# A fused window attention and two-layer network: the order of the first token tile's attention, its value products and its bank order

## The chip, the core and the metric

The kernel runs on one core of one Trainium2 chip. The core has five engines that each work through a queue of their own in order: TensorE (PE, matrix products; PEld in the profile is its weight load), VectorE (DVE), ScalarE (ACT), GpSimd (POOL) and SyncE (SP). They meet through semaphores. Data lies in SBUF, 128 partitions wide; products are written to PSUM, which the kernel uses as eight banks of 128 x 512 float32. DMA transfers are issued from POOL and SP (one from ACT at the very end). The metric is device time in microseconds (us) for one launch.

## The reference

Batch 8, 8 heads, 576 positions, 64 numbers a head. Each query sees the 64 keys up to and including its own position. The attention's output, 4608 rows of 512, goes through a layer of 2048 columns, `h * cos(h)`, and a layer back to 512.

```python
def _attn_ref(q, k, v):
    scores = scale * np.matmul(q, k.transpose(0, 1, 3, 2))
    rel = pos[:, None] - pos[None, :]
    mask = (rel >= 0) & (rel < 64)
    scores = np.where(mask, scores, -1000000000.0)
    ...
    return np.matmul(attn, v).astype(np.float32)

def _moe_ref(x, w_in, w_out):
    h = x @ w_in
    g = h * np.cos(h)
    return (g @ w_out).astype(np.float32)
```

## The kernel before

**Tiling.** The 4608 rows are cut into nine token tiles of 512 rows (`mt`). A tile's input `xT` (512 numbers deep, 512 rows wide, turned) comes from the attention as four slices, one for each pair of heads (`p` = 0 to 3). The first layer makes 16 column blocks (`ff`) of 128, each from four products of 128 x 128 by 128 x 512, one for each pair (`first`, line 351). ACT takes the cosine as a sine with an offset (line 519), DVE multiplies it with `h` (line 522), and the second layer sums 16 products for each 128 rows (line 534).

**Attention.** Queries come in blocks of 64 (`j` = 0 to 8). A block `j` needs the keys of blocks `j - 1` and `j`, so a unit is one pair and one block with 128 keys. The first token tile is batch 0, blocks 0 to 7. Its 32 units are handled in eight groups of four: group `p.g` is pair `p`, blocks `4g` to `4g + 3`. The steps of a group have letters, and so do the steps of a pair:

- `tq.p`, `tk.p`: 18 turns on PE each (line 186) of a pair's queries or keys into a PSUM tile of tag `t` (three buffers). `pq.p`, `pk.p`: its copy to SBUF on DVE (`d`) or ACT (`a`), lines 193 to 199.
- `s.p.g`: one product that lays the mask into a bank (line 238) and eight scores (line 244). `m`: the maximum, negated, on DVE (line 273). `e`: four exponentials with their sums on ACT, read from the score bank itself (line 288). `i`: the reciprocal on DVE (line 295). `n`: the multiply into weights `w` on POOL (`p`) or DVE (`d`), line 302.
- `w.p.g`: four turns of the weights on PE into a `t` tile (line 311); `c.p.g`: its copy to SBUF (`wT`).
- `v.p`: 16 products of weights and values (line 330) into a `t` tile; `x.p`: its copy into `xT`.
- `z.half`: the spread of the values. They are loaded in chunks of 128 rows into the even ones of eight slots. A block with odd `j` finds its two key blocks in one slot, `j - 1`. A block with even `j` needs the upper half of one chunk and the lower half of the next; for it the odd slots are filled by two copies, `z.1` (upper halves, POOL) and `z.0` (lower halves, DVE).
- `l`: the next of seven loads on POOL: three parts of `w_in`, `q` and `k` of batch 1, two halves of `w_out`.
- `h.p`: the share of pair `p` in the first three column blocks, `hx.f`: pairs 0 and 1 of column block `f`, `hl`: pairs 2 and 3 of the first five column blocks. `tb` loads the sine table on ACT.

**What sets the order.** The string `FIRST` (lines 41 to 48) is the order by hand of everything up to the first layer of tile 0; line 490 walks through it and issues each step to its engine's queue. Behind it come the loads of batch 0's last values and batch 1's values (lines 493 to 495). Then the loop over the tiles runs from line 497, and a plan with due times (`at`, `pump`) puts the attention of the next batches between the products. The turns of batch 1's `q` and `k` are due at 7 to 12.7 (lines 424 to 427), from the eighth column block of tile 0 on.

**Banks.** Five PSUM banks have names (O0, O1, X0, X1, S), three are the tag `t`. `S_FIRST` (line 101) names the banks of the scores in turn, and `H_FIRST` (line 96) those of the 16 column blocks of tile 0. A bank is used again only when the last reader of its contents is done. `skew(mt)` is the number of column blocks that are begun before all four pairs are there: five for tiles 0 and 1, three (`SKEW`) for the others.

Of the kernel before, what the change touches and what calls it, by code (L numbers as in the profile page):

```python
# [10 lines left out]
def _safe_warn(msg, *a, **kw):  # L11
# [14 lines left out]
GF = 4  # L26
# [25 lines left out]
def kernel(  # L52
# [43 lines left out]
    H_FIRST = ("O1", "X0", "X1", "S", "O0") * 3 + ("X0",)  # L96
# [208 lines left out]

    def g_trans(n):
# [27 lines left out]

    def put_x(mt, p, engine=None):
# [18 lines left out]
    def skew(mt):  # L354
        return 5 if mt < 2 else SKEW
# [118 lines left out]
    def load():  # L474
# [7 lines left out]
             "mk": put_masks, "ck": lambda: cast("k", "d"), "l": load, "tb": sine_table, "h": lambda p: skewed(0, p, next(turn_h)), "hl": lambda: last_pairs(0),  # L482
             "hx": lambda ff: [first(0, ff, ks, ks == 0, False) for ks in range(2)],
             "z": lambda half, engine=None: spread_v(0, half, engine),
# [3 lines left out]
             "c": lambda p, g, engine=None: g_put(2 * p + g, engine), "v": lambda p: values(0, p),  # L488
# [4 lines left out]
    load_v(0, 4)  # L493
    for c in range(5):
        load_v(1, c)
# [81 lines left out]
```

## Time and profile before

| | us |
|---|---|
| three runs | 305.22, 307.27, 306.64 |
| median | 306.64 |
| the profiled execution, its time | 306.41 |
| its span, first to last instruction | 304.4 |
| PE busy in the span | 288.7 (95%) |
| ACT busy | 235.7 (77%) |
| DVE busy | 220.4 (72%) |
| POOL busy | 171.1 (56%) |

The page divides the span into 40 slices of 7.6 us and gives each engine's busy tenths there. A row of the timeline has the start, the length, the engine, the line, the operation, what it writes and reads with shapes, and how many were merged; in brackets is the engine's idle time ahead of it and what ended that. A row of a group has the count, the time in all, the mean in ns, and the idle time ahead. A row of DMA issues has the queue, the count, the size and the median time to landing. By windows, the profile gives each engine's busy time in a stretch, with the granted clock of PE, from 0 to 1, near its end. The window 30 to 40 us has PE busy for 9.44 of 10 us, the windows of 50 us behind 50 us for 49.4 to 49.5.

### The profile page before, as it was taken

Reading aid. Unit: us, or ns where it says so; the run is one execution under the profiler, and the core shown is the slowest. Engines: PE = TensorE matmul, PEld = TensorE weight load, DVE = VectorE, ACT = ScalarE, POOL = GpSimd, SP = SyncE. Lnnn points to the kernel's source line nnn. Section 1 sums busy time; section 2 is a strip of 40 time slices with the busy share of each in tenths; the row PEclk is TensorE's granted clock in tenths of the full one; section 3 lists DMA queues with packets and bytes.
Section 4 is the critical chain, followed back from the end, with each engine's and each line's share of the span. In section 5 each row is a group of like instructions: output and inputs, shape, how many; then the busy total and the mean of one; then the engine's idle time right before and its main releaser. Section 6 shows DMA issues by size and latency. Waiting matters only on the chain.

```text
span 304.4 us, 7847 instructions
## 1 busy us (share of the span) xinstructions
PE 288.7 (95%) x2628; PEld 142.1 (47%) x2668; DVE 220.4 (72%) x834; ACT 235.7 (77%) x786; POOL 171.1 (56%) x198
## 2 busy tenths in 40 slices
PE   3769999999999999999999999999999999999996
PEld 3544444544454445444544444444444454454443
DVE  3896889588787878787877787778778877236701
ACT  5997799967997799779987998799869986106600
POOL 8996257977774976497659665967433630000000
PEclk9989999999999999999999999999999999999999
DMA  7999999699969999999999979999994441011012
GB/s 150 181 211 207 207 155 139 105 165 191 225 114 155 225 164 132 154 201 183 138 167 208 189 106 172 157 219 123 180 172 110 87 130 62 0 72 70 0 69 71
DMA packets 165577, 43.88 MB, mean 144 GB/s; under 512 B 154720, under 2 KB 160800, under 8 KB 165536
## 3 DMA queue, kind: packets, MB, share of 16 engines
q0 software_dynamic: 99344, 18.06, 75.1%
q1 hardware_dynamic: 66048, 25.11, 40.2%
q8 instruction: 21, 0.34, 0.5%
q14 instruction: 20, 0.16, 0.2%
q10 hardware_dynamic: 144, 0.20, 0.2%
HBM read 36.70 MB, written 9.44 MB: 152 GB/s over the span
## 4 chain that ended last, share of the span: by engine, by line
PE 88%; DVE 6%; issue 2%; ACT 2%; DMA 1%; POOL 0%; DVEq 0%; POOLq 0%
PE h_ps L351 41%; PE out_ps L534 36%; PE o_ps L330 3%; PE s_ps L261 3%; DVE negm L273 1%; PE out_ps L371 1%; DMA first_f<-in_q_dram 1%; DVE w L302 1%; PE tq_ps L186 1%; DVE s L277 1%; DVE v L109 1%; PE tk_ps L186 1%; PE tw_ps L311 1%; PE s_ps L244 1%; ACT e L288 1%
## 5 line engine op out<-in xcount | busy, mean ns | idle before, releaser
L351 PE MATMUL h_ps<-xT,w_in 128*128 128x512 bf16 x556 | 127.1, 381 | 2.2 <-DVE xT L109 0.6
L534 PE MATMUL out_ps<-w_out,gT 128*128 128x512 bf16 x543 | 123.0, 379 | 1.8 <-issue 1.1
L522 DVE TENSOR_TENSOR gT<-h_ps,sin 128x512 bf16<-128x512 f32 x144 | 95.4, 688 | 33.6 <-ACT sin L519 33.4
L519 ACT ACTIVATE sin<-h_ps 128x512 f32<-128x512 f32 x144 | 82.9, 599 | 34.1 <-PE h_ps L351 32.8
L288 ACT ACTIVATE e<-s,negm 128x128 f32<-128x128 f32 x256 | 98.6, 388 | 0.3 <-DVE negm L277 0.3
L302 POOL TENSOR_TENSOR w<-e,rden 128x512 bf16<-128x512 f32 (+1 forms) x76 | 74.5, 993 | 31.5 <-DVE rden L295 29.1
L351 PEld LDWEIGHTS <-w_in 128*128 128x128 bf16 x576 | 56.0, 98 | 67.1 <-issue 2.7
L534 PEld LDWEIGHTS <-gT 128*128 128x128 bf16 x560 | 53.2, 98 | 62.4 <-issue 0.2
L277 DVE CUSTOM_DVE_ANT_0 s<-s_ps,mask 128x128 f32<-128x128 f32 x256 | 58.0, 284 | 0.1
L288 ACT ACTIVATION_READ_ACCUMULATOR e<-s,negm 128x1 f32 x256 | 48.1, 188 | 0.0
L149 POOL DMA_DIRECT2D rows<-in_q_dram x30 | 25.4, 867 | 25.9 <-DMA T<-rows 16.6
L162 POOL DMA_DIRECT2D v<-in_v_dram x35 | 29.8, 879 | 10.5 <-DMA rows<-in_k_dram 7.3
L109 ACT COPY out_sb<-out_ps 128x512 f32<-128x512 f32 (+1 forms) x18 | 10.1, 563 | 24.2 <-PE out_ps L534 18.7
L295 DVE RECIPROCAL rden<-den 128x4 f32<-128x4 f32 (+1 forms) x80 | 13.8, 172 | 19.2 <-ACT e L288 18.6
L149 POOL DMA_DIRECT2D rows<-in_k_dram x30 | 25.5, 897 | 2.2 <-DMA T<-rows 2.2
L109 DVE CAST xT<-o_ps 128x512 bf16<-128x512 f32 x27 | 17.6, 679 | 6.5 <-PE o_ps L330 6.3
L277 DVE DVE_READ_ACCUMULATOR2_ANT negm<- 128x1 f32 x256 | 21.2, 83 | 0.0
L109 DVE COPY out_sb<-out_ps 128x512 f32<-128x512 f32 x18 | 12.4, 689 | 12.0 <-PE out_ps L534 12.0
L288 ACT ACTIVATE e<-s_ps,negm 128x128 f32<-128x128 f32 x32 | 11.5, 425 | 1.6 <-DVE negm L273 1.6
L261 PE MATMUL s_ps<-T 64*64 64x128 bf16 x512 | 12.1, 221 | 0.0
L261 PEld LDWEIGHTS <-T 64*64 64x64 bf16 x512 | 8.2, 106 | 8.3 <-DVE negm L277 4.4
L330 PEld LDWEIGHTS <-v 128*64 128x64 bf16 x504 | 9.5, 112 | 4.3 <-issue 2.1
(56 smaller groups left out, 146.2 us busy)
## 6 DMA issues: line engine op xcount, KB each, us to landing
out_dram<-out_sb SPq DMA_DIRECT2D x16, 512.0 KB, 6.1
v<-in_v_dram POOLq DMA_DIRECT2D x28, 128.0 KB, 8.3
rows<-in_q_dram POOLq DMA_DIRECT2D x24, 128.0 KB, 5.2
rows<-in_k_dram POOLq DMA_DIRECT2D x24, 128.0 KB, 7.8
w_out<-in_moe_w_out_dram POOLq DMA_DIRECT2D x2, 1024.0 KB, 16.7
w_in<-in_moe_w_in_dram POOLq DMA_DIRECT2D x2, 768.0 KB, 12.4
wT<-w SPq DMA_TRANSPOSE x66, 3.9
out_dram<-out_sb SPq DMA_DIRECT2D x3, 256.0 KB, 2.0
```

The lines of the kernel that those rows point to most:

```text
L109: {"a": nc.scalar.copy, "p": nc.gpsimd.tensor_copy}.get(engine, nc.vector.tensor_copy)(out, in_)
L149: nc.gpsimd.dma_start(out=rows(b)[lo:lo + n, slot * 512:slot * 512 + 512].rearrange("p (h d) -> p h d", h=H), in_={"q": q, "k": k}[name][b ...
L162: nc.gpsimd.dma_start(out=vt.rearrange("p (h d) -> p h d", h=H), in_=v[b, :, c * 128:c * 128 + n, :].rearrange("h p d -> p h d"))
L261: nc.tensor.matmul(out=s_ps[cross][to, u].rearrange("p (a t) -> p a t", a=2), lhsT=q_cols(b, p, j)[d], rhs=k_cols(b, p, j)[d], start=True, ...
L277: nc.vector.tensor_tensor_reduce(out=s[:, u], in0=s_ps[:, u], in1=mask[:, 2 - j % 2 if j else 0], scale=-scale if b else -1.0, scalar=BIG, ...
L288: nc.scalar.activation(e[:, u], s[:, u], AF.Exp, bias=negm[:, u:u + 1], scale=1.0 if n < n_first else -1.0, accum_out=den[:, u:u + 1])
L302: (nc.gpsimd if engine == "p" else nc.vector).tensor_tensor(out=w[:, 0:u], in0=e[:, 0:u], op=ALU.mult, in1=rden[:, 0:u].unsqueeze(2).to_br ...
L330: nc.tensor.matmul(out=o_ps[64 * h:64 * h + 64, 64 * i:64 * i + 64], lhsT=values_of(b)[:, max(j - 1, 0), 128 * p + 64 * h:128 * p + 64 * h ...
L351: nc.tensor.matmul(out=st["h", ff], lhsT=w_in_sb[:, ks, ff * 128:ff * 128 + 128], rhs=st["xT", mt][:, ks], start=start, stop=stop)
L519: nc.scalar.activation(sin, h_ps, AF.Sin, bias=math.pi / 2.0)
L522: nc.vector.tensor_tensor(out=gt[:, e], in0=h_ps, in1=sin, op=ALU.mult)
L534: nc.tensor.matmul(out=o_ps[e], lhsT=gT[ff // 2][:, ff % 2, ms * 128:ms * 128 + 128], rhs=w_out_sb[:, ff], start=ff == 0, stop=ff == n_ff - 1)
```

## The change

The order `FIRST` is written anew. What else changes belongs to steps in it:

- `warm.24` stands first: 24 products of the identity with itself (128 x 128 by 128 x 128) into bank X1, which nothing reads.
- Both scores, maxima and exponentials of pair 0 come ahead of pair 1's copies; before, `s.0.1 tq.1 tk.1 s.0.0` and `m.0.0` came later.
- `pk.3` and `c.1.0` go from ACT to DVE, `c.2.0` too; `n.1.0` from DVE to POOL; `x.0` from DVE to ACT. Of `n.3.1` DVE makes three units and POOL the fourth (`nh`).
- The loads `l` are issued at other places: one as before, two behind `n.0.1`, the last four behind `nh.3.1`.
- Values of pairs 0 and 1 don't use the odd slots: `va.p` makes the products of the odd blocks from one slot, as before, and those of the even blocks with the lower half; `vb.p` adds the even blocks' upper half from the chunk before. That is 24 products for a pair and not 16. They go to banks X0 and S and not to a `t` tile. The spread `z` covers pairs 2 and 3 alone, half the columns, and `spread_last` copies slot 7's upper half for pairs 0 and 1 behind the loads of `l`, for tile 1.
- `h` begins two column blocks and not three, `hx` one and not two, `hl` ends three and not five, and `H_FIRST` has another order for the first ten column blocks.
- `tb` moves from behind `w.3.1` to behind the last copy into `xT`.

```diff
 FIRST = (
-    "tq.0 mk ck tk.0 pq.0.d pk.0.a s.0.1 tq.1 tk.1 l s.0.0 m.0.1 pq.1.d tq.2 e.0.1 pk.1.d s.1.0 pq.2.a "
-    "tk.2 s.1.1 i.0.1 tq.3 l m.0.0 m.1.0 pk.2.d n.0.1.p s.2.0 l w.0.1 tk.3 s.2.1 e.0.0 l e.1.0 m.1.1 "
-    "l i.0.0 e.1.1 pq.3.d i.1.0 m.2.0 pk.3.a e.2.0 n.0.0.p n.1.0.d z.1.p w.0.0 i.1.1 m.2.1 e.2.1 "
-    "s.3.0 s.3.1 c.0.1.d n.1.1.p c.0.0.d w.1.0 m.3.0 i.2.0 z.0.d c.1.0.a n.2.0.p w.1.1 c.1.1.d v.0 "
-    "i.2.1 v.1 n.2.1.p m.3.1 e.3.0 e.3.1 l x.0.d w.2.0 i.3.0 x.1.d h.0 c.2.0.a n.3.0.p w.2.1 h.1 hx.3 "
-    "i.3.1 n.3.1.d w.3.0 c.2.1.a w.3.1 tb v.2 c.3.0.d x.2.a c.3.1.d v.3 l x.3.d hx.4 hl "
+    "warm.24 tq.0 mk ck tk.0 pq.0.d pk.0.a s.0.1 s.0.0 tq.1 tk.1 l m.0.1 e.0.1 m.0.0 e.0.0 pq.1.d tq.2 tk.2 pk.1.d "
+    "s.1.0 pq.2.a s.1.1 i.0.1 n.0.1.p l l m.1.0 e.1.0 tq.3 pk.2.d i.0.0 n.0.0.p s.2.0 w.0.1 m.1.1 e.1.1 tk.3 s.2.1 "
+    "pq.3.d i.1.0 n.1.0.p z.1 m.2.0 pk.3.d e.2.0 w.0.0 i.1.1 n.1.1.p m.2.1 e.2.1 "
+    "c.0.1.d s.3.0 s.3.1 z.0 i.2.0 n.2.0.p m.3.0 e.3.0 c.0.0.d w.1.0 va.0 i.2.1 n.2.1.p m.3.1 e.3.1 w.1.1 "
+    "c.1.0.d i.3.0 n.3.0.p c.1.1.d w.2.0 w.2.1 c.2.0.d va.1 vb.0 i.3.1 nh.3.1 l l l l x.0.a c.2.1.a w.3.0 "
+    "c.3.0.d w.3.1 c.3.1.d h.0 vb.1 x.1.d v.2 x.2.a v.3 h.1 hx.2 x.3.d tb hl "
 )
...
-    H_FIRST = ("O1", "X0", "X1", "S", "O0") * 3 + ("X0",)
+    H_FIRST = ("O1", "X0", "O0", "S", "X1") * 2 + ("O1", "X0", "X1", "S", "O0", "X0")
...
+    def spread_pairs(half):
+        vt = values_of(0)[:, :, d_model // 2:]
+        if half:
+            nc.gpsimd.tensor_copy(vt[64:128, 1:8:2], vt[64:128, 0:7:2])
+        else:
+            nc.vector.tensor_copy(vt[0:64, 1:7:2], vt[0:64, 2:8:2])
+
+    def spread_last():
+        vt = values_of(0)[:, :, 0:d_model // 2]
+        nc.gpsimd.tensor_copy(vt[64:128, 7], vt[64:128, 6])
...
+    def g_norm_halves(n):
...
+        for engine, lo, hi in ((nc.vector, 0, 3), (nc.gpsimd, 3, 4)):
+            engine.tensor_tensor(out=w[:, lo:hi], in0=e[:, lo:hi], op=ALU.mult,
+                                 in1=rden[:, lo:hi].unsqueeze(2).to_broadcast([128, hi - lo, 128]))
...
+    def warm(n):
+        to = bank("X1", "none_ps")
+        for _ in range(n):
+            nc.tensor.matmul(out=to[:, 0:128], lhsT=ident, rhs=ident, start=True, stop=True)
+
+    def values_first(p, part):
+        if part == "a":
+            st["o", 0, p] = bank(("X0", "S")[p], "o_ps")
+        lower, upper, both = slice(0, 64), slice(64, 128), slice(0, 128)
+        parts = {"a": [(lower, j, j) for j in range(0, TU, 2)] + [(both, j - 1, j) for j in range(1, TU, 2)],
+                 "b": [(upper, max(j - 2, 0), j) for j in range(0, TU, 2)]}[part]
...
     def skew(mt):
-        return 5 if mt < 2 else SKEW
+        return 5 if mt == 1 else SKEW
...
-        for ff in range(skew(mt) if mt else SKEW):
+        for ff in range(skew(mt) if mt else 2):
...
     load_v(0, 4)
+    spread_last()
     for c in range(5):
         load_v(1, c)
```

More of the change, by code (lines that the diff above doesn't have):

```diff
@@ L304, in g_norm @@
         st["w", n] = w
+    def g_norm_halves(n):
+        (e, _), rden = st.pop(("e", n)), st.pop(("r", n))
+        w = att.tile([128, GF, 128], BF16, tag="w", name="w", bufs=8)
+        for engine, lo, hi in ((nc.vector, 0, 3), (nc.gpsimd, 3, 4)):
+            engine.tensor_tensor(out=w[:, lo:hi], in0=e[:, lo:hi], op=ALU.mult,
+                                 in1=rden[:, lo:hi].unsqueeze(2).to_broadcast([128, hi - lo, 128]))
+        st["w", n] = w
     def g_trans(n):
@@ L332, in values @@
                                  rhs=wT[:, 64 * (h ^ cross):64 * (h ^ cross) + 64], start=True, stop=True, skip_group_check=True)
+    def warm(n):
[8 more added lines that the diff above has]
+                 "b": [(upper, max(j - 2, 0), j) for j in range(0, TU, 2)]}[part]
+        for i, (ks, slot, j) in enumerate(parts):
+            for h in range(2):
+                nc.tensor.matmul(out=st["o", 0, p][64 * h:64 * h + 64, 64 * j:64 * j + 64],
+                                 lhsT=values_of(0)[ks, slot, 128 * p + 64 * h:128 * p + 64 * h + 64],
+                                 rhs=st["wT", (0, p, j)][ks, 64 * h:64 * h + 64],
+                                 start=part == "a" and i == 0, stop=True, skip_group_check=True)
     def put_x(mt, p, engine=None):
@@ L487 @@
              "n": lambda p, g, engine: g_norm(2 * p + g, engine), "w": lambda p, g: g_trans(2 * p + g),
-             "c": lambda p, g, engine=None: g_put(2 * p + g, engine), "v": lambda p: values(0, p),
+             "c": lambda p, g, engine=None: g_put(2 * p + g, engine), "va": lambda p: values_first(p, "a"), "vb": lambda p: values_first(p, "b"), "v": lambda p: values(0, p),
+             "z": spread_pairs,
              "x": lambda p, engine=None: put_x(0, p, engine)}
```

4 lines of the change are left out of this document (2 added, 2 removed).

## The prediction

> **What bounds the kernel now.** I read the page first: its span, and TensorE and its clock in 40 slices.
>
> ```profile
> span 304.4 us, 7847 instructions
> PE   3769999999999999999999999999999999999996
> PEclk9989999999999999999999999999999999999999
> ```
>
> TensorE (PE) is full from the fifth slice on; only the first three, some 23 us, have holes, and the change edits little else. So I went to the chain of waits (start, length, what), for where the full stretch begins.
>
> ```profile
> 20.59 0.59 PE h_ps L351
> 24.64 0.61 PE o_ps L330 x24
> 25.74 0.59 PE h_ps L351 x2
> 26.36 4.69 PE h_ps L351 x21
> ```
>
> From 26.36 the first-layer products run back to back, 4.69 / 21 = 0.22 us apart. The first token tile needs 64 of them. Ten stand ahead of `hl` in the old order (3 in each `h`, 2 in each `hx`), so 54 are left at 26.36. The question is when the new order starts its dense run, and with how many left. Then I read the front in the timeline, engine by engine.
>
> ```profile
> 7.73 0.37 ACT L288 ACTIVATE e<-s_ps,negm 128x128 f32<-128x128 f32 x1 [1.45 <-DVE negm L273]
> 9.82 0.65 ACT L197 ACTIVATE T<-tq_ps 128x576 bf16<-128x576 bf16 x1 [0.58 <-PE tq_ps L186]
> 10.36 0.36 ACT L288 ACTIVATE e<-s_ps,negm 128x128 f32<-128x128 f32 x1
> 14.47 0.71 ACT L109 COPY T<-tk_ps 128x576 bf16<-128x576 bf16 x1
> 17.73 0.72 ACT L109 COPY wT<-tw_ps 128x512 bf16<-128x512 bf16 x1
> 21.42 0.59 ACT L109 COPY wT<-tw_ps 128x512 bf16<-128x512 bf16 x1
> 11.58 0.81 POOL L175 DMA_DIRECT2D w_in<-in_moe_w_in_dram  x1
> 12.38 0.75 POOL L142 DMA_DIRECT2D rows<-in_q_dram  x1
> 13.11 0.76 POOL L142 DMA_DIRECT2D rows<-in_k_dram  x1
> 13.87 1.07 POOL L302 TENSOR_TENSOR w<-e,rden 128x512 bf16<-128x512 f32 x1
> 15.00 2.25 POOL L109 COPY v<-v 64x2048 bf16<-64x2048 bf16 x1
> 21.46 1.06 POOL L302 TENSOR_TENSOR w<-e,rden 128x512 bf16<-128x512 f32 x1
> 13.96 1.53 DVE L302 TENSOR_TENSOR w<-e,rden 128x512 bf16<-128x512 f32 x1
> 21.79 1.29 DVE L302 TENSOR_TENSOR w<-e,rden 128x512 bf16<-128x512 f32 x1
> 25.62 0.69 DVE L109 CAST xT<-o_ps 128x512 bf16<-128x512 f32 x1 [0.41 <-PE o_ps L330]
> ```
>
> ScalarE (ACT) makes the exponentials of eight groups between 7.73 and 21.42. Twelve of them lie without a gap between 10.36 and 14.47, 0.343 apart, so 32 take 11.0. GpSimd (POOL) has its first weights done early but starts `n.0.0` only at 13.87, behind three transfers, and later carries the 2.25 us spread. From the last exponential (21.4) to the last `xT` cast's end (26.3) are 4.9 us. That tail and the two queues ahead of it are what the change rewrites.
>
> **ACT's queue.** Ahead of the last exponential the old order has 11.0 of exponentials, `pq.2` (0.65), `pk.3` (0.71), `c.1.0` (0.72) and a 0.58 wait. The change takes `pk.3` and `c.1.0` to VectorE (DVE) and puts `e.0.0` in the wait. Left are 11.0 + 0.65, so the last exponential ends at 7.73 + 11.65 = 19.4, if no maximum is late.
>
> **DVE's queue.** It takes those two, and `c.2.0`, and gives away `n.1.0`, a quarter of `n.3.1`, half of `z.0` and one cast of `xT`.
>
> ```profile
> L273 DVE TENSOR_REDUCE negm<-s_ps 128x4 f32<-128x512 f32 x8 | 5.4, 672 | 1.7 <-PE s_ps L244 1.7
> L199 DVE TENSOR_SCALAR T<-tq_ps 128x576 bf16<-128x576 bf16 x3 | 2.2, 743 | 0.3 <-PE tq_ps L186 0.3
> L109 DVE COPY wT<-tw_ps 128x512 bf16<-128x512 bf16 x5 | 1.9, 416 | 1.4 <-PE tw_ps L311 1.4
> L109 DVE COPY v<-v 64x1536 bf16<-64x1536 bf16 x1 | 1.5, 1482 | 0.0
> L295 DVE RECIPROCAL rden<-den 128x4 f32<-128x4 f32 x8 | 1.4, 170 | 0.6 <-ACT e L288 0.6
> ```
>
> From `m.0.1` (7.0; its result fed the exponential at 7.73) to `m.3.1` it now has eight maxima (5.4), five copies of turned rows (3.7), two of `wT` (0.8), half a spread (0.75) and six reciprocals (1.0): 11.7, so 18.7 at full lengths one behind the other. The exponentials of `3.1` could begin at 19.4 - 1.4 = 18.0. So the cover is thin: between nothing and 0.7 goes to ACT. I take the middle, 0.3, and the last exponential ends at 19.7.
>
> **POOL's queue.** Weights `0.1` can start at 9.8: their reciprocal stands behind two maxima and two copies, 7.0 + 2 x 0.67 + 2 x 0.74. Then come 1.05 of multiply and two transfers of 0.81, so 12.5. From there six multiplies at 1.06 and the half spread, 2.25 / 2 = 1.1, end at 20.0. So POOL, not ACT, releases the last group, 2.5 us before the old `n.3.0` ended (21.46 + 1.06). `n.3.1` follows: three quarters on DVE, one on POOL. In the old trace DVE's multiplies stretched to 1.53 and 1.29, and both ended 0.55 after POOL's own multiply did (15.49 against 14.94, 23.08 against 22.52). So DVE stood still until POOL was through and then needed 0.55. I price the split in series: 0.27 + 0.75 x 0.55 = 0.7, ending at 20.7; its ends are 0.41 (side by side) and 1.15 (three quarters of 1.53). The Trainium skill, "SBUF — State Buffer", section "SBUF: two separate sides", says that a DVE operation with two SBUF inputs and a GpSimd operation reading SBUF take a shared port pair as an exclusive lock. It speaks against this split: by it DVE alone would need 0.55 and the split at least as much, whereas a shared bandwidth would give 0.41.
>
> **The tail on PE.** After `w.3.1` PE runs, in its order: `h.0` (2 products), `vb.1` (8), `v.2`, `v.3` (16 each), `h.1`, `hx.2` (2 each), then `hl`.
>
> ```profile
> 21.83 0.63 PE L311 MATMUL tw_ps<-ident,w 128*128 128x128 bf16 x4
> 22.25 1.94 PE L351 MATMUL h_ps<-xT,w_in 128*128 128x512 bf16 x5
> 24.57 1.01 PE L330 MATMUL o_ps<-wT,v 128*64 128x64 bf16 x32
> 16.83:20.24 3.41, 1.68 (x42) 1.22 (x41) 3.41 (x7) 3.23 (x18) 3.33 (x4) 1.00 1.16 211
> 20.24:23.65 3.41, 2.84 (x10) 1.40 (x11) 2.43 (x5) 2.91 (x11) 3.39 (x5) 0.50 1.17 210
> ```
>
> The last two rows are windows (length, PE, PEld, DVE, ACT, POOL, granted clock, DMA share, GB/s). After the thin window to 20.24, with only 1.68 us of PE work, the clock stood at 0.50 for 3.41 us, and first-layer products came 0.43 apart, turns 0.42 / 4 = 0.105. In the new order the scores end near 16 (`pk.3` ends on DVE near 14.6, two groups follow at 0.64), and until 20.2 PE has five turns (2.0), `va` twice and `vb.0` (40 small products, 1.01 / 32 = 0.03 each, 1.2): as thin, so I take the slow clock again from about 20.2. Then `w.3.1` runs 20.7 to 21.1, `h.0` to 22.0, `vb.1` and `v.2` to 22.8, `v.3` to 23.3, the last cast (0.69) to 24.1, while `h.1` and `hx.2` go on to 24.3 as the clock returns. `hl` starts at 24.3, with 6 done and 58 left: four more than before, 4 x 0.22 = 0.9. So 24.3 + 0.9 = 25.2 stands against 26.36: **1.2 us gained**.
>
> **What lies beside.**
>
> ```profile
> 1.02 0.29 POOL masks.py:199 TENSOR_SCALAR_AFFINE_SELECT ident<-ident 128x128 bf16<-128x128 bf16 x1
> 4.43 0.69 PE L186 MATMUL tq_ps<-ident,rows 64*64 64x64 bf16 x18 [4.43 <-ACT rows L109]
> ```
>
> The halves add 16 products, 0.5 us; `va` sits in PE's idle time, `vb.1` is in the tail above; without that cover they cost 0.5. The sine table now follows `x.2` on ACT, and the first sine comes near 25.0, still ahead of PE's need of that bank five column blocks on. `hl` over three columns and the other bank order change no count. The last spread of slot 7 sits on POOL behind the loads, with only batch 1's values behind it. SP issues nothing that moves. The 24 identity products can start when the identity is done, at 1.3, take 24 x 0.105 = 2.5, and end before the first turn's rows come at 4.43. If weight loads don't overlap they take twice that, 5.0, and delay the first turn by 1.9.
>
> **A faster first part** I price at nothing, between 0 and 0.46.
>
> ```profile
> 8.66 0.64 PE L244 MATMUL s_ps<-T 64*64 64x128 bf16 x8 [0.47 <-issue]
> 10.15 0.41 PE L244 MATMUL s_ps<-T 64*64 64x128 bf16 x8
> ```
>
> Eight scores took 0.64 before 10 us and 0.41 after: 0.23 for each slow step, two of which stand ahead of 7.73. The Trainium skill, "TensorE: Matmul & The Clock Gate", Part 1, asks for about 3.4 us of sustained work before the clock rises; the 2.5 us alone don't give that, and by it this term is nil or partial.
>
> **Transfers moved on POOL.** `q` and `k` of batch 1 go from 12.38 and 13.11 to behind `n.3.1`, some 20.4 and 21.2.
>
> ```profile
> rows<-in_q_dram POOLq DMA_DIRECT2D x1, 576.0 KB, 15.4
> rows<-in_k_dram POOLq DMA_DIRECT2D x1, 576.0 KB, 17.5
> DMA to landing us min/median/max: 7.8/11.5/13.4
> 30.98 0.48 PE L186 MATMUL tq_ps<-ident,rows 64*64 64x64 bf16 x36
> ```
>
> `q` landed at 27.8, `k` at 30.6, the last third of `w_in` (the third row, its longest) at 11.58 + 13.4 = 25.0: 2.8 apart, 576 KB at 208 GB/s, as the windows have it. So they stood in a full queue, and an issue at 20.4, well ahead of 25.0, lands them when it did. PE turns them after the eighth column block, 26 products behind 24.3, now near 29.8: cover is left.
>
> **Rivals.** (1) *The clock stays up in the tail.* For it: PE starts earlier and the counts are near the edge. Then `h.0`, `h.1` and `hx.2` cost 0.22 each, `hl` starts at 23.4, and 2.1 are gained: 304.3 for this execution. (2) *DVE becomes the bound.* It gains 0.75 + 0.42 of ACT's work, and six reciprocals stand ahead of maxima, each waiting on ACT. If that 1.2 comes back, nothing is left: 306.4. The change not doing what it says (the slow first turn above is 1.9 against 1.2) ends near the same, at 307. (3) *Slower: the rows of batch 1 come late.* If the landing is counted from the issue, `q` comes at 20.4 + 15.4 = 35.8 and the turn, in PE's own order at 29.8, holds everything 6.0 us; less 1.2, 4.8 lost: 311.2. It decides once the queue runs dry, with the issue later than about 23 (25.0 less 2), and hurts past the 2 us between 27.8 and 29.8. Against it stands the even spacing. (4) *All low ends together:* rival 1, the 0.46 of the first part, and 0.3 each from DVE not waiting and the split side by side: 3.2 gained, 303.2.
>
> **The numbers.** The profiled execution took 306.41 us, its span 304.4 and 2.0 around it; the median of the three runs is 306.64 (305.22 to 307.27), 0.2 more. The forecast is 306.41 - 1.2 = 305.2 by the execution, and 305.4 by the median. Chances: forecast 0.42, rival 1 0.22, rival 2 with its kin 0.16, rival 3 0.08, rival 4 0.12. One per cent (3.07 us) is about what a measurement of this kernel can tell from no change. Faster by more takes rival 4 and, as runs differ by 2 us, a part of rival 1: 0.18. Slower is rival 3, 0.08. Within: 0.74. The range leaves out rival 3 and the far end of rival 4, and takes in the spread of runs: 303.3 to 307.3.
>
> **What would show it.** In the changed profile: the last exponential ends near 19.7; POOL's multiplies from 12.5 to 20 without a transfer among them; the clock at 0.50 once near 20 to 24 (forecast) or not (rival 1); the dense run of first-layer products starting near 24.3; batch 1's first turn with no wait for `rows`. A maximum that ACT waits for in mid-front shows rival 2. A dense run after 25.5, or a hole ahead of batch 1's turns, makes the forecast wrong.

## The result, and the profile after

| | before | after |
|---|---|---|
| median of 20 runs, us | 306.58 (305.22 to 307.66) | 307.98 (306.36 to 311.77) |
| ratio after to before | | 1.0055, 95% interval 1.0036 to 1.0074 |
| the profiled execution, its time, us | 306.41 | 307.97 |
| its span, us | 304.4 | 305.8 |

The change made the kernel slower by 0.55%. The ratio leaves out one slow run, the one of 311.77 us; the medians of the table alone would give 1.0046. The forecast was 305.4 us, 0.4% faster, and 307.98 lies outside its range of 303.3 to 307.3.

The page of the changed kernel, whose first slices have fewer holes than before:

```profile
span 305.8 us, 7935 instructions
...
PE   7879998999999999999999999999999999999996
PEclk9989999999999999999999999999999999999999
```

The timeline of the front, in the form of the prediction's rows (start, length, engine, line, tiles, count, idle time ahead). First POOL from its first weights on, then the last exponential, the split and the dense run:

```profile
11.31 1.56 POOL L186 DMA_DIRECT2D w_in<-in_moe_w_in_dram  x2
12.87 2.06 POOL L313 TENSOR_TENSOR w<-e,rden 128x512 bf16<-128x512 f32 x2
19.48 0.50 ACT L299 ACTIVATE e<-s_ps,negm 128x128 f32<-128x128 f32 x1
20.32 0.56 DVE L321 TENSOR_TENSOR w<-e,rden 128x384 bf16<-128x384 f32 x1
20.36 0.77 POOL L321 TENSOR_TENSOR w<-e,rden 128x128 bf16<-128x128 f32 x1 [0.22 <-DVE rden L306]
23.78 0.69 DVE L109 CAST xT<-o_ps 128x512 bf16<-128x512 f32 x1 [0.30 <-PE o_ps L349]
25.63 4.70 PE L388 MATMUL h_ps<-xT,w_in 128*128 128x512 bf16 x21
30.26 0.48 PE L197 MATMUL tq_ps<-ident,rows 64*64 64x64 bf16 x36
20.24:23.65 3.41, 3.34 (x56) 2.11 (x50) 2.14 (x5) 1.37 (x3) 3.29 (x5) 0.50 1.13 199
```

The front does what the change says. No transfer lies any more between POOL's multiplies, the last exponential ends at 20.0, the last cast at 24.5, and the 21 first-layer products that stood at 26.36 stand at 25.63. Batch 1's first turn (`tq_ps`) begins at 30.26 without a wait, where it began at 30.98. So some 0.7 us are won at 30 us, and the kernel is nevertheless longer in the end.

Where they go is seen by following one mark through the token tiles. These are the starts of the first second-layer product (`out_ps`) of each of the first four tiles, in the two traces, and the span:

```
            tile 0   tile 1   tile 2   tile 3   span
before       40.97    74.25   105.14   136.01   304.4
after        40.25    74.83   105.80   137.39   305.8
difference   -0.72    +0.58    +0.66    +1.38    +1.4
```

Two stretches lose time, one between tiles 0 and 1 (1.30 us) and one between tiles 2 and 3 (0.72 us). The others are equal within 0.1. PE's waits in the changed trace (in total, times, longest) name both. In the kernel before, PE waited for no turned weights, and all its waits for POOL's weights lay in the front:

```profile
PE tw_ps L330 <- POOL w L313: 1.2, 1, 1.2
PE o_ps L349 <- DMA wT<-w: 0.6, 1, 0.6
```

**The first loss**, near 50 us. The timeline of the kernel before, and then of the changed one, in the same stretch:

```profile
45.72 1.81 POOL L149 DMA_DIRECT2D rows<-in_k_dram  x2
48.68 0.16 DVE L295 RECIPROCAL rden<-den 128x3 f32<-128x3 f32 x1
49.00 0.82 POOL L302 TENSOR_TENSOR w<-e,rden 128x384 bf16<-128x384 f32 x1 [1.46 <-PE s_ps L261]
49.87 0.34 PE L311 MATMUL tw_ps<-ident,w 128*128 128x128 bf16 x3
```

```profile
46.83 2.48 POOL L149 DMA_DIRECT2D rows<-in_k_dram  x3
47.95 0.17 DVE L306 RECIPROCAL rden<-den 128x3 f32<-128x3 f32 x1
49.38 1.61 POOL L313 TENSOR_TENSOR w<-e,rden 128x384 bf16<-128x384 f32 x2
50.26 0.34 PE L330 MATMUL tw_ps<-ident,w 128*128 128x128 bf16 x3 [1.21 <-POOL w L313]
```

POOL's multiply of a group of three units waits for two things: its reciprocal (`rden`), which is through 7.87 us after the mark of tile 0 in both traces (48.84 - 40.97 and 48.12 - 40.25), and the loads of batch 2's rows that stand ahead of it in POOL's queue. Before, the loads were through at 47.53, POOL stood idle for 1.46, and the reciprocal came last. After, the loads are through at 49.31 and come last. Before, they had a cover of 48.84 - 47.53 = 1.31. The front takes 0.72 of it by being earlier, the loads 1.78 by being later, and 0.72 + 1.78 - 1.31 = 1.19, where PE waits 1.21.

The loads are later because those of batch 1 were issued later, into a queue that ran thinner (runs 1 and 2 below test this). Here are the list of transfers of the changed kernel (KB each, us to landing; 15.4 and 17.5 before), a row of POOL that was at 28.08 before, and the windows (GB/s last) that were at 204, 210, 206 and 206 GB/s:

```profile
rows<-in_q_dram POOLq DMA_DIRECT2D x1, 576.0 KB, 8.8
rows<-in_k_dram POOLq DMA_DIRECT2D x1, 576.0 KB, 10.5
22.00:24.00 2.00, 2.00 (x42) 1.43 (x43) 0.91 (x3) 0.63 (x2) 2.00 (x3) 0.59 1.11 180
24.00:26.00 2.00, 1.95 (x10) 0.89 (x10) 0.50 (x2) 1.99 (x4) 1.96 (x4) 1.00 1.16 176
26.00:28.00 2.00, 2.00 (x11) 0.88 (x9) 2.00 (x4) 1.73 (x4) 2.00 (x3) 1.00 1.22 212
28.00:30.00 2.00, 2.00 (x11) 0.88 (x9) 1.78 (x3) 1.47 (x3) 0.11 (x1) 1.00 1.14 183
30.16 0.88 POOL L162 DMA_DIRECT2D v<-in_v_dram  x1 [2.06 <-DMA rows<-in_q_dram]
```

The `q` rows, issued at 21.08, land at 21.08 + 8.80 = 29.88, where they had landed at 27.80. (The landing of the part of `w_in` ahead of them stands in no row of this trace; before, it was at 24.93.) The loads behind them stay some 1.8 us late, since POOL, before each issue, waits for the landing of the load eight issues earlier, as the row at 30.16 does for `q`: `w_out` lands at 42.52 for 40.74, and the first row of batch 2 is issued at 37.99 for 36.20. In each of the 17 traces of this case that issue comes 0.53 or 0.54 behind the landing of the first half of `w_out`, so a late landing there moves everything that is queued behind it on POOL.

**The second loss**, near 122 us. PE's timeline of the values of batch 3 in the kernel before and in the changed one:

```profile
120.45 1.04 PE L330 MATMUL o_ps<-wT,v 128*64 128x64 bf16 x54
121.53 1.67 PE L351 MATMUL h_ps<-xT,w_in 128*128 128x512 bf16 x6
```

```profile
120.75 1.13 PE L349 MATMUL o_ps<-wT,v 128*64 128x64 bf16 x46
122.49 0.47 PE L349 MATMUL o_ps<-wT,v 128*64 128x64 bf16 x18 [0.62 <-DMA wT<-w]
```

PE waits for the last of the weights that DMA turns (`wT<-w`, issued by SP). Before, the last two took 2.47 and 2.42 us from issue to landing (the last landed at 120.34). After, they took 3.91 and 3.86, and the last landed at 122.45, though it was issued 0.67 later only. The change touches nothing there. What moved in the trace is another transfer. The page counts the packets of instructions, here of the queue that run 10 shows to be PE's (packets, MB, share of the time of the 16 DMA engines):

```profile
q8 instruction: 21, 0.34, 0.5%
```

That is 0.34 MB / 21 = 16 KB for each. In the changed trace one begins at 117.9, among the six turns, and takes 1393 ns; in the kernel before the nearest two begin at 109.3 and 123.9. PE executes 80 instructions more than before (24 identity products and 16 halves, each with its weight load), so the packets of its code fall at other places. Over all 17 traces the two go together: the five with a packet between 116.9 and 120.3 (the change, runs 1, 3, 4 and 6) wait 0.36 to 1.68 for `wT<-w` between 121 and 124, the other twelve 0.28 or less.

### The profile page after: what moved, and what is told of

It is laid out like the page before. It is cut to its first block, busy times and chain, and to the rows that moved or that the text cites. A ratio compares the mean times of both kernels' runs of the same rounds, so it can differ in the third digit from the quotient of the medians.

```text
span 305.8 us, 7935 instructions
## 1 busy us (share of the span) xinstructions
PE 292.3 (96%) x2669; PEld 145.6 (48%) x2708; DVE 218.4 (71%) x835; ACT 234.9 (77%) x784; POOL 171.7 (56%) x201
## 4 chain that ended last, share of the span: by engine, by line
PE 78%; ACT 9%; DMA 4%; DVE 3%; issue 3%; POOL 2%; POOLq 0%; DVEq 0%
PE h_ps L388 41%; PE out_ps L573 28%; ACT e L299 7%; PE o_ps L349 3%; DMA wT<-w 3%; PE s_ps L272 2%; POOL w L313 2%; PE out_ps L408 1%; DMA first_f<-in_q_dram 1%; ACT L380 1%; DVE s L288 1%; ACT sin L558 1%; PE s_ps L255 1%; PE tq_ps L197 1%; PE tw_ps L330 1%
## 5 line engine op out<-in xcount | busy, mean ns | idle before, releaser
L388 PEld LDWEIGHTS <-w_in 128*128 128x128 bf16 x576 | 55.8, 98 | 65.7 <-issue 0.6
L349 PE MATMUL o_ps<-wT,v 128*64 128x64 bf16 x472 | 10.7, 200 | 0.8 <-DMA wT<-w 0.6
```

The source lines that it names most:

```text
L349: nc.tensor.matmul(out=o_ps[64 * h:64 * h + 64, 64 * i:64 * i + 64], lhsT=values_of(b)[:, max(j - 1, 0), 128 * p + 64 * h:128 * p + 64 * h ...
L388: nc.tensor.matmul(out=st["h", ff], lhsT=w_in_sb[:, ks, ff * 128:ff * 128 + 128], rhs=st["xT", mt][:, ks], start=start, stop=stop)
```

## The experiments

Each ratio below is to the kernel before, measured in the same rounds, with its 95% interval in brackets.

The theory that the first four runs tested: the rows of batch 1, issued late, shift POOL's loads, and PE pays for it near 50 us. Its rivals put the loss into the front itself (the clock, the identity products). That the code packets make the second loss was the theory of the runs behind them, when the first four had shown that loss where the late rows had no hold on it.

**Run 1: the rows of batch 1 early again.** The changed kernel, with `q` and `k` back behind the last part of `w_in`:

```diff
- ... n.0.1.p l l m.1.0 ... nh.3.1 l l l l x.0.a ...
+ ... n.0.1.p l l l l m.1.0 ... nh.3.1 l l x.0.a ...
```

> The changed kernel with one edit: q and k of batch 1 are issued on POOL right behind the w_in loads (near 12.9 and 13.7 us) and not behind the last multiply (21.1). Theory A (late transfers): the queue no longer runs thin at 22 to 26 us, q lands near 28 and not 30, w_out's second half near 41, POOL's first load for batch 2 is issued near 36 and not 38, and PE's wait of 1.2 us near 49 goes. POOL's weights of the first tile come up to 1.5 us later, so the dense run starts at 24.6 to 25.6 and not 24.1. Time: 306.0 to 306.8, ratio to before 0.998 to 1.001. Theory B (bank order and fewer column blocks begun early cost the time): stays at 1.004 or more, and PE still waits near 49.

Measured: 308.16 us median, ratio 1.0071 (1.0044 to 1.0098). The queue is restored, with `q` landing at 28.1, and the wait near 50 is gone. But the time did not come back. POOL's timeline shows what was given up for it:

```profile
10.79 1.56 POOL L186 DMA_DIRECT2D w_in<-in_moe_w_in_dram  x2
12.33 0.77 POOL L142 DMA_DIRECT2D rows<-in_q_dram  x1
13.06 0.78 POOL L142 DMA_DIRECT2D rows<-in_k_dram  x1
13.81 2.08 POOL L313 TENSOR_TENSOR w<-e,rden 128x512 bf16<-128x512 f32 x2
```

Two issues of 0.77 ahead of the next multiply put it at 13.81 in place of 12.87, and the mark of tile 0 is at 41.10. The clock's slow stretch lay later as well in this trace (21.36 to 24.77), but the traces of runs 7 and 8, with loads ahead of the multiplies too, have the mark at 41.91 and 42.11, and the six of the new front without them at 39.7 to 40.8. So the front's gain goes with those issues. A wait of 0.4 for `wT<-w` near 121 stays. The run confirms the cause of the wait near 50 and refutes that undoing it helps.

**Run 2: the rows late in the kernel before.** The four loads behind `n.3.1.d`, and nothing else:

```diff
- ... e.0.0 l e.1.0 m.1.1 l i.0.0 ... e.3.1 l x.0.d ... n.3.1.d w.3.0 ... v.3 l x.3.d ...
+ ... e.0.0 e.1.0 m.1.1 i.0.0 ... e.3.1 x.0.d ... n.3.1.d l l l l w.3.0 ... v.3 x.3.d ...
```

> The kernel before with one edit: q and k of batch 1 and w_out are issued on POOL behind its last multiply of the first tile. Theory A: the queue runs thin, everything behind it lands 2 us late or more, PE waits for batch 1's rows near 31 or for weights near 50: ratio 1.003 to 1.010. Theory B: nothing of the products' order changes, and POOL's early weights come sooner: 0.997 to 1.001.

Measured: 307.42, ratio 1.0039 (1.0017 to 1.0060). Late loads alone cost 0.4%, some 70% of what the change cost. The timeline near 49 of this kernel:

```profile
45.77 2.48 POOL L149 DMA_DIRECT2D rows<-in_k_dram  x3
46.94 0.17 DVE L295 RECIPROCAL rden<-den 128x3 f32<-128x3 f32 x1
48.22 1.67 POOL L302 TENSOR_TENSOR w<-e,rden 128x384 bf16<-128x384 f32 x2
49.17 0.34 PE L311 MATMUL tw_ps<-ident,w 128*128 128x128 bf16 x3 [1.14 <-POOL w L302]
```

The loads end at 48.25, 1.14 behind the reciprocal, and PE waits 1.14. This profiled execution took 305.64, the lowest of its twelve, since its front was early (mark of tile 0 at 39.23, with the clock's slow stretch from 17.8 to 21.2); there is no wait near 121.

**Run 3: the change without the identity products** (`warm.24` left out).

> The changed kernel without the 24 identity products. If they do nothing, as the slow scores up to 10.0 us say: the clock rises at the same 10.0 us, and the time is that of the changed kernel within 0.5 us (ratio 1.003 to 1.007). If they help: the first scores come later and the time is 0.5 us or more above the changed kernel's.

Measured: 309.46, ratio 1.0105 (1.0079 to 1.0130), worse than the change itself. The front did not move (mark of tile 0 at 40.36), but PE's waits grew at both places:

```profile
PE tw_ps L330 <- POOL w L313: 2.4, 2, 1.8
PE o_ps L349 <- DMA wT<-w: 1.7, 1, 1.7
```

Forty-eight instructions fewer on PE, and the packet that had begun at 117.9 begins at 120.3, takes 1519 ns and falls on the sixth turn. Nothing in the front explains a wait at 122. This was the first sign that the length of PE's stream matters, and it speaks against the identity products as a cause by their own time.

**Run 4: a later due time.** The changed kernel, with two `k` loads of batch 2 behind POOL's first multiplies:

```diff
-             at(t0 - T + ((19.4 if c < 2 else 28.6) + 0.01 * c if b == 2 else 10.5 + 0.9 * c) if c < 4 else
+             at(t0 - T + ((23.4 if c < 2 else 28.6) + 0.01 * c if b == 2 else 10.5 + 0.9 * c) if c < 4 else
```

> The changed kernel with the due time of two loads of batch 2's k moved from 19.4 to 23.4, behind three of POOL's multiplies of batch 1. Theory A: the transfers stay late (first load for batch 2 near 38), but the multiply that PE waited for is no longer queued behind those loads: it starts near 48.3 and not 49.4, PE's wait of 1.2 us near 49 falls to 0.3 or less, and 0.5 to 1.0 us are won (307.0 to 307.5), unless batch 2's turns then come late. Theory B: the wait near 49 stays, the time is the changed kernel's.

Measured: 307.66, ratio 1.0053 (1.0032 to 1.0074). The wait near 50 is gone (0.4 near 56 is left) and the time is as it was. Its trace waits 0.8 for `wT<-w` near 121, so this alone left open whether the first loss was worth nothing or was replaced; run 12 bears on that.

**Runs 5 and 6: the code packets, moved on purpose.** A helper of 64x64 identity products in PE's idle start, 112 of them in the changed kernel in the place of the 24, and 40 in the kernel before:

```diff
+    def small_products(n):
+        to = bank("X1", "none_ps")
+        for i in range(n):
+            d = slice(64 * (i % 2), 64 * (i % 2) + 64)
+            nc.tensor.matmul(out=to[d, 0:64], lhsT=ident[d, d], rhs=ident[d, d], start=True, stop=True, skip_group_check=True)
...
-    "warm.24 tq.0 mk ...
+    "small.112 tq.0 mk ...
```

> The changed kernel, with 112 identity products of 64x64 in the place of the 24 of 128x128 at PE's start: 176 instructions of PE more, so that every later instruction of PE stands 256 places behind where it stood in the kernel before, plus none. Theory (the 16,384-byte instruction packets that feed PE moved with the length of its stream and fell among the weight turns of batch 3): the packet that took 1393 ns at 117.94 is back near 124, PE waits nothing over 0.1 us at 121 to 122, and the stretch from the third tile's first second-layer product to the fourth's is 30.9 us, not 31.59; against the changed kernel about 0.7 us is won (ratio to the kernel before near 1.003). The wait of about 1.2 us near 50 stays, since the rows of batch 1 and 2 are issued where they were. Rival (the wait at 121 comes from the later loads, or from chance): 31.5 us in that stretch and a wait of 0.5 to 0.9 us, ratio 1.0055.

> The kernel before, with 40 identity products of 64x64 at PE's idle start: 80 instructions of PE more, as many as the changed kernel has, and nothing else. Theory (instruction packets): a packet falls at about 117 to 118, among the six weight turns of batch 3, the last turns land about 3.9 us after issue in place of 2.4, PE waits 0.5 to 1.0 us near 121, ratio 1.002 to 1.003. Rival (the length of the stream does nothing): no wait there, 30.87 us from the third to the fourth tile, ratio 1.000.

Measured: run 5, 306.69, ratio 1.0024 (1.0006 to 1.0043); run 6, 306.62, ratio 1.0028 (1.0012 to 1.0045). Lengthening PE's stream by the change's 80 instructions costs the kernel before 0.28%, and with that shift taken out the changed kernel stands 0.31% lower (1.0055 less 1.0024). PE's waits of run 6, where the kernel before had none for `wT<-w`:

```profile
PE o_ps L330 <- DMA wT<-w: 1.8, 3, 1.0
60.47 0.41 PE L330 MATMUL o_ps<-wT,v 128*64 128x64 bf16 x14 [0.99 <-DMA wT<-w]
```

Three batches are hit, for the packets stand at 55.8, 87.1 and 118.0, each among a batch's turns; the fourth turn of batch 1, for one, took 5.37 us to land in place of 2.44. In run 5 the packets stand at 123.5 and 50.5, as in the kernel before. Its PE goes from values to first layer without a hole, and near 49 its loads end 0.07 ahead of the reciprocal:

```profile
119.91 1.04 PE L349 MATMUL o_ps<-wT,v 128*64 128x64 bf16 x54
120.99 1.89 PE L394 MATMUL h_ps<-xT,w_in 128*128 128x512 bf16 x8
```

```profile
46.41 1.81 POOL L149 DMA_DIRECT2D rows<-in_k_dram  x2
48.12 0.17 DVE L306 RECIPROCAL rden<-den 128x3 f32<-128x3 f32 x1
48.46 0.82 POOL L313 TENSOR_TENSOR w<-e,rden 128x384 bf16<-128x384 f32 x1 [0.24 <-PE s_ps L272]
49.34 0.34 PE L330 MATMUL tw_ps<-ident,w 128*128 128x128 bf16 x3
```

That execution took 306.06. The expectation that the wait near 50 stays was wrong for it: the `q` rows, issued at 20.59, landed at 27.64, no later than in the kernel before, and the first half of `w_out` 0.48 later only (36.15 for 35.67; 37.46 in the changed kernel's trace).

**Run 7: both losses taken away**, run 1's order with the 112 small products.

> The changed kernel with the q and k loads of batch 1 back right behind w_in, and the 112 small products in the place of the 24. Theory (both losses: late rows, and instruction packets): no wait near 49 to 50 and none at 121; the first second-layer product stays at about 41.1, as POOL's multiplies go later by what it issues in front of them, so the time is that of the kernel before within 0.2%: ratio 1.000 to 1.002. Rival (a third loss that neither removes): ratio 1.004 or more with no wait over 0.3 us at both places.

Measured: 308.23, ratio 1.0074 (1.0053 to 1.0096): the rival's ratio. Neither place waits over 0.3, but the front is 0.9 later than before (mark of tile 0 at 41.91). What went with that in this trace stands in a window (length, PE, PEld, DVE, ACT, POOL, granted clock):

```profile
15.53:25.77 10.24, 9.71 (x126) 6.20 (x126) 7.32 (x16) 6.07 (x26) 10.05 (x13) 0.50 1.17 209
```

The clock was at one half for 10.24 us and not 3.41, over the whole tail of the front. All six timed executions of this kernel were granted 0.983 to 0.989 in the mean, those of the kernel before in the same rounds 0.987 to 1.000. That the loads ahead of POOL's multiplies bring this about was not shown; that the front comes later with them is (runs 1, 7 and 8).

**Run 8: one issue ahead of the multiplies only.** The second part of `w_in` ahead of `n.0.1`, `q` behind it, `k` and `w_out` behind the split, and the 112 small products:

```diff
- ... i.0.1 n.0.1.p l l m.1.0 ... nh.3.1 l l l l x.0.a ...
+ ... i.0.1 l n.0.1.p l l m.1.0 ... nh.3.1 l l l x.0.a ...
```

> The changed kernel with the second part of w_in and the q load of batch 1 issued by POOL before and just behind the first multiply of pair 0, k and w_out behind the split multiply, and the 112 small products in the place of the 24. Theory: the first second-layer product at 40.4 to 40.6, the queue without its gap of 5 us, no wait over 0.3 us near 50 nor at 121; so the half microsecond of the front is kept: ratio 0.998 to 0.999. Rival (the k load alone, behind the multiplies, is late enough to hold POOL's later loads): a wait of 0.5 to 1.2 us near 50 and ratio 1.001 to 1.003.

Measured: 307.53, ratio 1.0043 (1.0027 to 1.0060). No wait at either place, but POOL's first multiply moved to 11.04, its second to 13.58, the slow clock lasted from 19.5 to 26.3, and the mark of tile 0 came at 42.11 and not 40.5. Both theories were wrong on where it would lose.

**Runs 9 and 10: the due time once more, and the control of the packets.** Run 9 is run 5 with run 4's due time. Run 10 is the kernel before with 128 small products, 256 instructions, a whole packet.

> The changed kernel with the 112 small products in the place of the 24, and with the due time of two k loads of batch 2 moved from 19.4 to 23.4 us, so that POOL's multiply of batch 2 stands ahead of them: both losses are taken away and the front is as in the changed kernel. Theory (the 0.24% that stay with the small products alone are the wait near 50, in executions in which the loads land later than in the profiled one): ratio 0.997 to 1.000, no wait over 0.3 us near 50 nor at 121. Rival (the rest has another cause, in the front or the clock): ratio 1.002 to 1.004 as without the due time.

> The kernel before, with 128 identity products of 64x64 at PE's idle start: 256 instructions of PE more, which is one packet of 16,384 bytes at 64 bytes each, so the packets behind fall where they fell. A control for the 40 products, which cost 0.28%. Theory (it was the place of the packets): a packet at 123 to 124, no wait at 121, ratio 0.999 to 1.001. Rival (products in PE's idle start cost it by themselves, by the clock that they raise earlier): ratio 1.003 or more.

Measured: run 9, 307.85, ratio 1.0058 (1.0035 to 1.0080), above both of its theories, with a wait of 0.96 for turned rows near 75 in its trace; run 10, 306.14, ratio 1.0003 (0.9988 to 1.0018). Run 10 decides between its two theories for the packets: 256 instructions cost nothing where 80 cost 0.28%. Its trace has 22 packets, one more than before, with one at 122.9, and no wait near 121 (one of 0.5 for a later batch's turn, at 183).

**Runs 11 and 12: the due time with late loads, and alone**, both on the kernel before.

> The kernel before with the q, k and w_out loads behind POOL's last multiplies of the first token tile (1.0039 alone) and the due time of two k loads of batch 2 moved from 19.4 to 23.4 us. Theory (the late loads cost by the wait near 49 alone, for POOL's multiply that is queued behind batch 2's loads): the wait of 1.1 us is gone and the ratio is 1.000 or less, down to 0.997 if the earlier front of that trace (39.23 us for the first second-layer product, before 40.97) is of the order and not of the clock. Rival (lateness costs elsewhere as well): ratio 1.003 or more.

> The kernel before with the due time of two k loads of batch 2 moved from 19.4 to 23.4 us alone. A control: where nothing waits near 49, nothing is to be had, ratio 0.999 to 1.001; if the executions of the kernel before that take 306.5 us and more lie there by the same wait, 0.998.

Measured: run 11, 307.60, ratio 1.0037 (1.0019 to 1.0055); run 12, 308.08, ratio 1.0064 (1.0041 to 1.0087). The control was not neutral. PE's wait in run 12 shows why:

```profile
75.74 0.64 PE L261 MATMUL s_ps<-T 64*64 64x128 bf16 x32 [1.25 <-DMA T<-rows]
```

Rows that are loaded later are turned later, and batch 2's scores wait 1.25 for them. So the due time brings a wait near 75 in the traces of runs 9 and 12: it costs 0.64% where there is nothing to be had, 0.34% on run 5, and nothing on top of the late loads of run 2 or of the change. But the traces of runs 4 and 11 wait neither near 50 nor near 75 (0.4 near 56 to 57 is left), and their times did not come back. Run 11 has its rival's ratio: that the wait near 50 is all that late loads cost was not shown.

**Runs 13 to 15: the multiply on DVE.** The third multiply of batch 1 doesn't queue behind POOL's loads if DVE makes it (`if t or i > 2` for `i > 1` in the planner): on run 5, on the kernel before and on run 2.

> The changed kernel with the 112 small products (1.0024 alone), and the third multiply of batch 1's groups on VectorE in the place of POOL, so that it is not queued behind batch 2's loads. Theory (what is left is the wait near 49 to 50 in most executions): ratio 0.998 to 1.000, as the front's half microsecond is then kept. Rival (the rest is in the front or elsewhere): 1.002 to 1.003 as without it.

> The kernel before with the third multiply of batch 1's groups on VectorE: the control for the two others. Nothing waits there, VectorE takes 0.5 us more: ratio 0.999 to 1.002.

> The kernel before with the q, k and w_out loads late (1.0039 alone) and the third multiply of batch 1's groups on VectorE. Theory (late loads cost by the wait near 49 alone): no wait there, ratio 1.000 or less beside the control. Rival (lateness costs elsewhere as well, say by rows that land late): 1.003 to 1.004 as without it.

Measured: 307.28, ratio 1.0016 (0.9987 to 1.0046); 306.77, 1.0008 (0.9985 to 1.0031); 306.91, 1.0024 (0.9998 to 1.0050). Without the edit the ratios were 1.0024, 1 and 1.0039; the intervals overlap. The wait did not go, it went one multiply further (the late loads of run 15):

```profile
49.23 1.81 POOL L149 DMA_DIRECT2D rows<-in_k_dram  x2
51.00 1.68 POOL L302 TENSOR_TENSOR w<-e,rden 128x384 bf16<-128x384 f32 x2
51.95 0.34 PE L311 MATMUL tw_ps<-ident,w 128*128 128x128 bf16 x3 [1.29 <-POOL w L302]
```

The fourth multiply stands behind the same loads, which end at 51.04 here, and PE waits 1.29 for that one. The control, run 14, waits there too, 0.7, for a reciprocal that DVE gives later, so the edit brings a wait of its own and tells nothing on the price of the first loss.

The traces of runs 13 and 15 show one more price of late rows, one that lies ahead of the edit. PE waits for the `k` rows of batch 1, which land at 33.24 and 33.45 (30.61 before): 0.85 in run 13, whose front is that of run 5, and 0.98 in run 15.

```profile
33.28 0.48 PE L197 MATMUL tk_ps<-ident,rows 64*64 64x64 bf16 x36 [0.85 <-DMA rows<-in_k_dram]
```

**The rule of the first loss over the traces.** In each of the ten traces without the edits of runs 4, 9 and 11 to 15, the multiply near 49 starts within 0.2 us of the later of two times: the end of the loads ahead of it, and its reciprocal. Worked out from six of them, PE's wait beside the difference of the two (in the other four, runs 1, 7, 8 and 10, the loads end 1.1 to 2.7 ahead, and PE does not wait):

```
                     tile 0 mark   reciprocal   loads end   late by   PE waits
before                     40.97        48.84       47.53     -1.31        0
run 5                      40.41        48.29       48.22     -0.07        0
run 6                      39.76        47.63       47.43     -0.20        0
run 2                      39.23        47.11       48.25      1.14      1.1
changed                    40.25        48.12       49.31      1.19      1.2
run 3                      40.36        48.24       50.01      1.77      1.8
```

No version beat the kernel before. The nearest, with the change in it, are run 5 at 1.0024 and run 13 at 1.0016, which can't be told from no change (its median, 307.28, is 0.4% above the 306.02 of the kernel before).

## Why the prediction was wrong

**The front: right in its mechanism, its gain 0.7 and not 1.2.** The last exponential ended at 20.0 (forecast 19.7), POOL's multiplies ran from 12.87 to 20.14 (12.5 to 20.0), the clock was at 0.50 from 20.24 to 23.65, and the last cast ended at 24.5 (24.1). The number forecast as 25.2 against 26.36 came out as 25.63: 0.7 won and not 1.2. Of the 0.43 that are missing, 0.3 were there at the last exponential already, where the sum had taken the middle of its 0 to 0.7. With that, ACT and not POOL released the last group: POOL was free at 20.14, the reciprocal behind the last exponential was through at 20.29. This pair of executions had the same clock steps; in others the gain differs. The mark of tile 0 lay at 39.8 to 41.1 (40.6 in the mean) in the five traces with the old front and its loads in place (the kernel before, runs 6, 10, 12 and 14), and at 39.7 to 40.8 (40.4) in the six with the new one and its loads late.

**The split multiply: in series, as the sum had it.** The two rows look side by side (DVE 20.32 to 20.88, POOL 20.36 to 21.13), but POOL's quarter took 0.77, where a quarter of its 1.04 for a whole multiply is 0.26, and it ended 0.25 behind DVE's. In all nine traces with the split, POOL's end lies 0.25 to 0.26 behind DVE's, and DVE's three quarters took the same 0.56 in run 14, where POOL worked on nothing beside them. So POOL seems to have stood still until DVE was through. The row agrees with the lock that the Trainium skill states in "SBUF — State Buffer", "SBUF: two separate sides", as the prediction read it for this case: the split took 0.81 in all, more than the 0.55 that the prediction gave DVE alone. The price of 0.7 was 0.1 too low.

**The identity products: right as PE time, wrong as nothing else.** They ran from 1.37 to 4.11 (forecast 1.3 to 3.8), and the first turn was not delayed. The term of the faster first part was taken as nil, and in the changed trace it was: the granted clock rose at 10.0, and eight scores still took 0.63 at 7.39. In the traces of runs 1 and 4, with the same products, the clock rose at 4.29 and 4.98, and eight scores took 0.41 from 6.15 and 6.41 on. So what the Trainium skill's "TensorE: Matmul & The Clock Gate", Part 1, makes of 2.5 us of work (nil or partial) fits one trace of three; in run 1 the clock rose 2.9 us after the first of these products, less than its 3.4, in run 4 3.6 after it.

**What was left out of the sum: the code itself.** The change was counted as 0.5 us of halves and 2.5 us of identity products, both under cover. It also makes PE's stream 80 instructions longer. The forecast put that at nothing without a reason, and runs 6 and 10 give it 0.28% (0.9 us) for 80 instructions and nothing for 256.

**The failed step: the paragraph on transfers moved on POOL.** It said that "an issue at 20.4, well ahead of 25.0, lands them when it did", and rival 3 took the point where it decides to be "later than about 23 (25.0 less 2)". The 2 us of lead were no row of the trace. The issue came at 21.08, 3.9 ahead of 25.0, and the rows landed 2.1 later than before. How much later varies from one execution to the next, but the two sides don't overlap at the next load: in the eight traces with `q` issued early, `q` landed at 26.9 to 28.1 and the first half of `w_out` at 35.0 to 36.0; in the nine with `q` issued at 20.5 to 22.7, at 27.6 to 30.1 and 36.1 to 39.2. Rival 3 had the cause, but its trigger came too late in it and its price lay at the wrong place. The forecast followed the rows to PE's turn of batch 1, found cover there, and stopped. In the changed trace PE did not wait at 30.26, but in runs 13 and 15 it waits for the `k` rows near 33. And it should have followed the queue: everything behind on POOL shifts with it, up to the first multiply that PE waits for behind a load, where the cover was 1.31 and the front's own gain used 0.72 of it. Even with the loads in place, a front earlier by more than 1.31 would have met them there.

**What adds up.** By the profiled pair: -0.72 in the front, +1.30 to tile 1 (1.2 of it the wait near 50), +0.08, +0.72 to tile 3 (0.6 of it the wait for turned weights), nothing behind; +1.4, as the spans have it. By ratios: late loads 0.39% (run 2) and packets 0.28% (run 6) make 0.67%, for 0.55% measured. Each of the three has an interval of some 0.2% either way, so the 0.12% between them is no measure of what the front kept.

**What stays open.** Run 5 has neither wait in its profiled execution, which is the lowest of its twelve, and is still 0.24% slower in the median. That other executions wait near 50, or near 33 as run 13's does, is likely: the cover near 50 was 0.07, and the `q` rows landed anywhere from 27.6 to 30.1 with late issues. But no trace of such an execution of run 5 was seen, and the two edits that were to remove the wait near 50 brought waits elsewhere. No run takes the value products in halves, the bank order or the copies' new engines back one by one, so a part of the rest may be theirs. The packets aren't all of the second loss either: run 7 waits 0.3 and run 14 0.3 for `wT<-w` near 121 with packets at 123.4 and 122.2, and run 13 waits 0.6 at 90.7 with packets at 79.0 and 93.5. And the trace doesn't tell why a packet of 16 KB delays several turns by more than its own time.

## What to carry to other kernels

A transfer that moves behind other work lands later even when its issue still lies well ahead of the landing in front of it (3.9 us here), and what is queued behind it moves too. So take no lead for safe without a row that shows it, and follow the queue past the first consumer, to the place where an engine that PE waits for has a load ahead of its work. An earlier front uses up the cover behind it (0.72 of 1.31 here), so read the idle time of each engine at the later hand-overs before counting a gain. And added instructions can cost more than their time: where a DMA that PE waits for has little slack, try the same edit with a few dozen padding instructions more before judging it. One trace of a kernel is one draw: the clock's steps and the landings moved by a microsecond or two between executions of nearly the same code.

## What the runs showed of the hardware

PE's code came in packets of 16 KB, 21 or 22 in a span, which the page counts with the transfers of the DMA engines: two thirds of them took 0.9 to 1.0 us, the longest 2.1 (run 3), and 256 instructions of PE more made one packet more (run 10). Turns of weights by DMA beside such a packet landed 3.9 (the changed kernel), 4.8 (run 3) and 5.4 us (run 6) after their issue, where the last turns of a batch took 2.4 to 2.5 in the kernel before. In run 1, with a packet at 116.9, the last turn still took 2.46.

The granted clock moved in steps of 3.41 us. It fell 10.24 us (three steps) after its rise in ten of the 17 traces (10.0 and 20.24 in both kernels' own) and 13.65 or 17.07 after it in five; in run 6 it did not fall in the front, and run 13's trace has no change of it on record. Where it fell, it stayed at one half for 3.41, 6.83 or 10.24. In run 7 it stayed there for two more steps behind one that PE was busy for in full (15.53 to 18.94, 3.41 of 3.41 us). Which steps it hits varies from one execution to the next: with the old front, the mark of tile 0 is at 39.76 in run 6, without a slow stretch, and at 40.97 in the kernel before, which is as much as the whole change was to win.
